# A fused H3 convolution and GLU backward kernel: GLU scratch as contiguous token rows, and the last stage's TensorE work in 128x32 column tiles

## The chip, the cores and the metric

The kernel runs on one core of one Trainium2 chip. The metric is the device time in microseconds (us) of one execution. Three runs of the kernel before took 433.23, 432.94 and 431.38 us; the median is 432.94 us.

## What is computed

The reference is a forward function and its gradient. With 2048 tokens, 512 channels and a GLU width of 1376, the forward function is

```python
xn = layernorm(A_q)
k_shift[s] = sum over t < 4 of k[s - t] * shift_k[:, t]
kv  = k_shift * v
y   = causal_conv(kv, ssm_k) + kv * ssm_D       # by FFT of length 4096
out = A_q + xn * y + ((xn @ w_gate) * (xn @ w_up)) @ w_down
```

The kernel returns `out` and the gradients of the nine inputs for a given `grad_out` (called `go` below): those of q, k, v, the two convolution kernels, `D` and the three GLU weights. Everything is bfloat16, with float32 sums in PSUM.

## The kernel before

The 2048 tokens stand as 16 groups ("rows" r) of 128 partitions. The FFT is written as products with small tables, in three TensorE passes: `a_gen` (weights of 64 rows by 128 columns), `s_B` and `s_Bi` (64x32 and 32x64) and `last_dft` (128x64). Between the passes the data goes through two scratch tensors in device memory, `AX` and `CX`.

The GLU is cut into six steps j of 256 hidden units (one, j = 1, has 96). `mlp_rows` makes, for two token rows at a time, the three products that the gradients need: `h` for `out`, and the gradients of the gate and of the up branch. They lie in SBUF in a ring, 768 values a token (3 parts t of 256), and `dw_gen` makes the weights' gradients of them. The last stage needs the same values with hidden units on partitions, so they are transposed. There are two ways:

- most of them go to the scratch tensor `HD` by `hd_store` (line 440), and come back through DMA transposes issued by `hd_load` (line 616) into two buffers `hdP`, one for each pair of token rows n, in turn. The first four pairs fetch all of `HD`'s columns, the last four leave out one step's.
- step 5 and half of step 4 stay in SBUF and are transposed by TensorE in `turn_gen` (line 602), eight 128x128 blocks for each ScalarE copy back over the ring.

The last stage runs over n = 0..7, each two token rows. `last_dft` (line 693) multiplies what `c_load` (line 646) fetched from `CX` into the one buffer `f["C"]`; its three results go to `c_dkv`, `c_y` and `c_o5`. `c_dsk` (line 738) sums the gradient of the short filter over tokens with eight products of 32 columns. `y_o` (line 759) makes a token row of `out` in 11 products of 128x128 weights with 512 moving columns, and `y_x` (line 777) a row of the gradient of `xn` in 22. VectorE and ScalarE finish the rows, among others in `dk_pair` (the gradient of k).

The order of the work is fixed. Every call of an engine is recorded (class `Eng`, line 143; the recorded function is called in line 173, so the profile gives nearly every instruction this line). `emit` then issues the records in the order that a packed string, `PLAN`, gives, and the same string says which PSUM bank each result gets. Consecutive TensorE calls with the same PSUM bank form one record. All DMAs are issued by SyncE (SP) in one order, so a DMA behind a waiting one waits too. SP's part of the last stage for each n is, in this order: stores of results, `hd_load(n + 2)`, more stores, and the loads of x, k and v and `c_load`, with waits on VectorE, ScalarE and TensorE before many of them.

The DMA transposes of before read rows of 768 values:

```python
HD = dram.tile([R, 640, 768], BF, name="HD")            # line 70
hdP = [place([128, 6, 1152], BF, ...) for i in range(2)] # line 611
ldT(out=hdP[n % 2][:, :, 0:b - a], in_=HP[n, a:b])       # line 618
```

Of the kernel before, what the change touches and what calls it, by code (L numbers as in the profile page):

```python
# [10 lines left out]
BF = mybir.dt.bfloat16  # L11
# [7 lines left out]
D = 512  # L19
F = 1376  # L20
R = 16
NFB = 11
NST = 6
SW = [256, 96, 256, 256, 256, 256]
SF = [0, 1280, 256, 512, 768, 1024]
SB = [0, None, 1, 2, 3, 4]
WO = [12 * sum(SW[:j]) for j in range(NST)]
NCH = 8
KEEP = 8
# [4 lines left out]
KB = 1024  # L34
# [3 lines left out]
def kernel(  # L38
# [24 lines left out]
    nc = tc.nc  # L63
# [3 lines left out]
        return slice(c * 128, (c + 1) * 128)  # L67

    dram = ctx.enter_context(tc.tile_pool(name="dram", bufs=1, space=DRAM))
    HD = dram.tile([R, 640, 768], BF, name="HD")  # L70
    AX = dram.tile([128, 32, 3 * D], BF, name="AX")
    CX = dram.tile([8, 512 * 3 * D + 2048], BF, name="CX")[:, 0:512 * 3 * D]
    KS = dram.tile([128, 12, D], BF, name="KS")
# [66 lines left out]
    def fix(x):  # L140
        return x.at(x.slot.base) if isinstance(x, PV) else x

    class Eng:


        def __init__(self, name, real):
            self.name = name; self.real = real

        def __getattr__(self, meth):
            f = getattr(self.real, meth)  # L150

            def call(*a, **k):
                last = ops[-1] if ops else None
                own = []
                for x in list(a) + list(k.values()):
                    if isinstance(x, PV) and x.slot not in own:
                        own.append(x.slot)
                cols = k["rhs"].shape[-1] if meth == "matmul" and not isinstance(k["rhs"], PV) else 128
                if meth == "matmul":
                    cols = 1  # L160
                    for n in k["rhs"].shape[1:]:
                        cols *= n
                if self.name == "PE" and hold[0]:
                    o = hold[0][0]
                elif (self.name == "PE" and hold[0] is None and last is not None and last.eng == "PE" and last.slots == own
                      and last.cols + cols <= 2200 and last.prio == now[0]):
                    o = last
                else:
                    o = Op(self.name, now[0])
                    ops.append(o)  # L170
                    if self.name == "PE" and hold[0] is not None:
                        hold[0].append(o)
                o.fns.append(lambda: f(*[fix(x) for x in a], **{kk: fix(x) for kk, x in k.items()}))  # L173
                o.uses.append((meth, a, k))
                o.cols += cols
                for s in own:
                    if s not in o.slots:
                        o.slots.append(s)
            return call
# [20 lines left out]
    nc = NC  # L200
# [5 lines left out]
    MM = nc.tensor.matmul  # L206
    ld = nc.sync.dma_start
    st = nc.sync.dma_start
    ldT = nc.sync.dma_start_transpose

    def place(shape, dt, at):
        n = 1
        for s in shape[1:]:
            n *= s
        if dt == BF:
            v = big[0:shape[0], at // 2:at // 2 + n]
        else:
            v = big[0:shape[0], at // 2:at // 2 + 2 * n].bitcast(dt)
        if len(shape) == 3:
            return v.rearrange("p (a b) -> p a b", a=shape[1])  # L220
        if len(shape) == 4:
            return v.rearrange("p (a b c) -> p a b c", a=shape[1], b=shape[2])
        return v
# [23 lines left out]
    ident = rc.tile("ident", [128, 128])  # L247
    W12 = rc.tile("W12", [128, 192])
    W1 = W12[:, 0:128]
    W2 = W12[:, 128:192]  # L250
# [22 lines left out]
    def slot(j, r):  # L273
        return RH + 1536 * ((RO[j] + r) % RING)

    def ring(j, r, n=1):
        if j != 1:
            return place([128, n, 768], BF, slot(j, r)).rearrange("p r (t f) -> p r t f", t=3)
        return place([128, n, 384], BF, slot(1, 0) + 768 * r).rearrange("p r (t f) -> p r t f", t=3)[:, :, :, 32:128]
# [141 lines left out]
        TT(h[:, :, 1:3, :fw], d.to_broadcast((128, 2, 2, fw)), g[:, :, 0:2, :fw], op=ALU.mult)  # L421
        TT(h[:, :, 0, :fw], g[:, :, 0, :fw], g[:, :, 1, :fw], op=ALU.mult)

    HP = HD.rearrange("(n h) p e -> n (h p) e", h=2)

    def hd_at(b, odd):
        return 640 + 128 * b if odd else 128 * ((b + 1) % 4)

    def hd_store(j, r):
        if j == 1:  # L430
            st(HP[r // 2:r // 2 + 2, 512:640].rearrange("n p e -> p n e"), place([128, 2, 768], BF, slot(1, 0) + 768 * r))
        else:
            e, o = hd_at(SB[j], 0), hd_at(SB[j], 1)
            st(HP[r // 2, e:o + 128].rearrange("(h p) e -> p h e", p=128)[:, ::(o - e) // 128, :], ring(j, r, 2).rearrange("p r t f -> p r (t f)"))

    def skb(sk, j, n):
        return sk[:, j, :].unsqueeze(1).to_broadcast((128, n, D))
# [128 lines left out]
    f = {}  # L566
# [26 lines left out]
    def turn_gen():  # L593
        for j, r0 in ((NST - 2, R - KEEP), (NST - 1, 0)):
            blk = [(r, t, b) for r in range(r0, R) for t in range(3) for b in (0, 128)]
            for k in range(0, len(blk), 8):
                pt = bfv(rN(), 8, 128)
                for i, (r, t, b) in enumerate(blk[k:k + 8]):
                    nc.tensor.transpose(pt[:, i, :], ring(j, r)[:, 0, t, b:b + 128], ident[:])
                r, b = blk[k][0], k % 6  # L600
                ACOPY(place([128, 8, 128], BF, slot(j, r) + 256 * b), pt)
                yield
# [5 lines left out]
            for a, b in ((0, 6), (6, 11)):  # L608
                ld(wy[n][:, a:b, :], wy_d[:, i, a:b, :])

    hdP = [place([128, 6, 1152], BF, 109 * KB + 13824 * i) for i in range(2)]

    def hd_span(n):
        return (0, 1152) if 2 * n < R - KEEP else (128, 1024)

    def hd_load(n):
        a, b = hd_span(n)
        ldT(out=hdP[n % 2][:, :, 0:b - a], in_=HP[n, a:b])

    def hd_block(m, t, fb):  # L620
        h = hdP[m // 2 % 2]
        a = hd_span(m // 2)[0]
        if fb == 10:
            return h[:, 3 * (m % 2) + t, 512 - a:640 - a]
        if fb >= 8 or fb >= 6 and m >= R - KEEP:
            return place([128, 6, 128], BF, slot(fb // 2 + 1, m))[:, 2 * t + fb % 2, :]
        c = hd_at(fb // 2, m % 2) - a
        return h[:, 2 * t + fb % 2, c:c + 128]

    def f_alloc():  # L630
        m = Region(RA[0] + 8 * KB, RA[1])
# [62 lines left out]
    def last_dft(n):  # L694
        py = f["py"] = [v3(rF(), 2) for sig in range(3)]
        C = f["C"]
        together()
        for sig in (1, 0, 2):
            for rr in range(2):
                for h in range(2):  # L700
                    MM(py[sig][64 * h:64 * h + 64, rr, :], lhsT=W2, rhs=C[:, 2 * h + rr, sig * D:sig * D + D], start=True, stop=True)
        apart()

    def c_y(n):
# [54 lines left out]
    def y_o(n, rr):  # L759
        m = f["m"][n % 2]  # L760
        end = n == NCH - 1
        for c in (slice(0, 256), slice(256, 512)) if end and rr == 1 else (slice(0, 512),):
            po = rN("y")
            for fb in range(NFB):
                MM(po[:, c], lhsT=hd_block(2 * n + rr, 0, fb), rhs=wy["d"][:, fb, c], start=(fb == 0), stop=(fb == NFB - 1 and not end))
            if end:
                MM(po[:, c], lhsT=ident[:], rhs=m[:, rr, c], start=False, stop=True)
                ACOPY(m[:, rr, c], po[:, c])
            else:
                TT(m[:, rr, c], m[:, rr, c], po[:, c], op=ALU.add)  # L770
        if end:
            st(o0[:, 2 * n + rr, :], m[:, rr, :])
        elif rr == 1:
            st(o0[:, 2 * n:2 * n + 2, :], m[:])

    def y_x(n, rr):
        r = 2 * n + rr
        rs = slice(2 * n, 2 * n + 2)
        px = rN("y")
        for t, w in ((1, "g"), (2, "u")):  # L780
            for fb in range(NFB):
                MM(px, lhsT=hd_block(2 * n + rr, t, fb), rhs=wy[w][:, fb, :], start=(t == 1 and fb == 0), stop=(t == 2 and fb == NFB - 1 and n + 1 < NCH))
        e = t = f["e"][n % 2]; dxn = f["dxn"]
        if n + 1 == NCH:
            MM(px, lhsT=ident[:], rhs=e[:, rr, :], start=False, stop=True)
            nc.scalar.activation(dxn[:, rr, :], px, ACTF.Identity, accum_out=s1[:, r:r + 1])
        else:
            STT(dxn[:, rr, :], e[:, rr, :], 1.0, px, op0=ALU.mult, op1=ALU.add, accum_out=s1[:, r:r + 1])
        STT(e[:, rr, :], dxn[:, rr, :], 1.0, xn[:, r, :], op0=ALU.mult, op1=ALU.mult, accum_out=s2[:, r:r + 1])
        r1 = slice(r, r + 1)  # L790
        TS(c2[:, r1], s2[:, r1], -1.0 / D, None, op0=ALU.mult)
        STT(c1[:, r1], s1[:, r1], -1.0 / D, rstd[:, r1], op0=ALU.mult, op1=ALU.mult)
        STT(dxn[:, rr, :], xn[:, r, :], c2[:, r1], dxn[:, rr, :], op0=ALU.mult, op1=ALU.add)
        nc.scalar.activation(t[:, rr, :], dxn[:, rr, :], ACTF.Identity, bias=c1[:, r1], scale=rstd[:, r1])
        TT(t[:, rr, :], t[:, rr, :], go[:, r, :], op=ALU.add)
        if rr == 1:
            st(o1[:, rs, :], t[:])
# [112 lines left out]
    for n in range(NCH):  # L910
        last = n + 1 == NCH
        t = F0 + n * DF
# [138 lines left out]
```

## Time and profile before

| | |
|---|---|
| median of three runs | 432.94 us |
| span of the profiled execution, first to last instruction | 429.5 us |
| what lies around the span (median less span) | 3.4 us |
| TensorE busy | 419.6 us, 98% |
| VectorE busy | 352.8 us, 82% |
| ScalarE busy | 267.3 us, 62% |
| TensorE instructions | 3174 matmuls and 3174 weight loads |
| mean DMA rate | 290 GB/s |
| DMA packets | 94,878, of which 53,748 under 512 bytes |
| instruction fetch, queue q8 | 25 packets, 0.41 MB |

The profile is of one execution. A "span" is counted from its first instruction, and all times below are on that clock. In a group of the profile, `128*32` before a shape stands for the rows and columns of the weights that the instruction uses, and `128x512` for the partitions and elements that it streams or writes. PEld is the row of weight loads, which run beside the matmuls. SPq is SP's issuing of DMAs: an issue can last long, and nothing behind it is issued meanwhile.

### The profile page before, as it was taken

How to read it: one execution, taken by the hardware profiler on the slowest of the kernel's cores; microseconds unless marked ns; L12 is line 12 of the kernel's file. 1: busy time of each engine (PE TensorE's matmuls, PEld its weight loads, DVE VectorE, ACT ScalarE, POOL GpSimd, SP SyncE). 2: the span in 40 equal slices, each digit the busy share in tenths (PEclk: the TensorE clock that was granted, in tenths of full speed). 3: DMA queues.
4: the chain of work that ended last, by engine and by line, in shares of the span. 5: the costliest groups of instructions: out<-in, count | busy, mean ns of one | idle time of the engine just before them, and what ended most of it. 6: DMA issues, size and time to landing. Idle time of an engine off the chain costs nothing.

```text
span 429.5 us, 8151 instructions
## 1 busy us (share of the span) xinstructions
PE 419.6 (98%) x3174; PEld 204.1 (48%) x3174; DVE 352.8 (82%) x684; ACT 267.3 (62%) x374; POOL 3.5 (1%) x9
## 2 busy tenths in 40 slices
PE   7999999999999999999999999889999999999996
PEld 4665455754454333544444344444444544444443
DVE  6799979998549989899999981044869989999996
ACT  2986879698554998988989963664244340313323
POOL 1000000000000000000000000000000000000000
PEclk9999999999999999999999999999999999999999
DMA  7997787959796979989989989999999999999933
GB/s 249 401 405 240 281 305 264 370 214 381 295 338 200 322 274 306 316 254 338 321 250 315 340 282 254 241 363 336 265 290 267 310 256 317 306 282 301 284 150 124
DMA packets 94878, 124.65 MB, mean 290 GB/s; under 512 B 53748, under 2 KB 63865, under 8 KB 93816
## 3 DMA queue, kind: packets, MB, share of 16 engines
q1 hardware_dynamic: 94840, 124.13, 91.7%
q8 instruction: 25, 0.41, 0.4%
q14 instruction: 13, 0.11, 0.1%
HBM read 57.10 MB, written 54.04 MB: 259 GB/s over the span
## 4 chain that ended last, share of the span: by engine, by line
PE 91%; DMA 6%; DVE 1%; SPq 1%; issue 1%; ACT 0%; ACTq 0%
PE PP L173 91%; DMA big<-CX 4%; DMA big<-in_goT_dram 1%; DVE big L173 1%; SPq L173 1%; ACT big L173 0%; ACTq L173 0%
## 5 line engine op out<-in xcount | busy, mean ns | idle before, releaser
L173 PE MATMUL PP<-big 128*128 128x512 bf16 (+9 forms) x3174 | 419.6, 347 | 5.8 <-issue 1.8
L173 PEld LDWEIGHTS <-big 128*128 128x128 bf16 (+5 forms) x3174 | 204.1, 98 | 221.0 <-issue 65.2
L173 DVE TENSOR_TENSOR big<-big 128x1024 bf16<-128x1024 bf16 (+4 forms) x465 | 269.3, 629 | 46.0 <-ACT big L173 42.6
L173 ACT CAST big<-PP 128x512 bf16<-128x512 f32 (+2 forms) x314 | 225.2, 780 | 90.0 <-PE PP L173 74.8
L173 ACT ACTIVATE big<-big 128x512 bf16<-128x512 f32 (+3 forms) x30 | 19.1, 645 | 40.8 <-DVE big L173 40.8
L173 DVE CAST big<-PP 128x512 bf16<-128x512 f32 (+1 forms) x37 | 32.3, 873 | 11.9 <-PE PP L173 10.0
L173 ACT COPY big<-PP 128x1024 bf16<-128x1024 bf16 x25 | 24.9, 1019 | 21.5 <-PE PP L173 21.5
L173 DVE SCALAR_TENSOR_TENSOR big<-big 128x1 f32<-128x1 f32 (+2 forms) x52 | 25.5, 498 | 0.6 <-ACT big L173 0.2
L173 DVE BATCH_NORM_STATS2 big<-big 128x6 f32<-128x512 bf16 x16 | 10.8, 679 | 2.7 <-DMA big<-in_x_dram 2.6
L173 DVE TENSOR_TENSOR big<-big,PP 128x512 bf16<-128x512 bf16 x14 | 9.5, 682 | 4.1 <-PE PP L173 4.0
L173 DVE SCALAR_TENSOR_TENSOR big<-big,PP 128x512 f32<-128x512 bf16 x14 | 9.5, 682 | 3.3 <-PE PP L173 3.3
L173 DVE TENSOR_SCALAR big<-big 128x1 f32<-128x1 f32 (+1 forms) x28 | 7.0, 259 | 0.2
L173 POOL MEMSET big<- 128x1536 bf16 (+2 forms) x3 | 2.8, 950 | 256.0 <-PE PP L173 252.7
L173 ACT ACTIVATE big<-PP 128x512 f32<-128x512 f32 x2 | 1.2, 598 | 5.5 <-PE PP L173 5.5
L173 DVE RECIPROCAL big<-big 128x2 f32<-128x2 f32 (+1 forms) x9 | 1.4, 155 | 3.7 <-ACT big L173 3.7
L173 DVE BATCH_NORM_AGGREGATE big<-big 128x2 f32<-128x6 f32 x16 | 2.8, 177 | 0.2
L173 ACT ACT_TABLE_LOAD x1 | 1.3, 1283 | 0.7 <-PEq L1039 0.7
L173 DVE DVE_READ_ACCUMULATOR big<-big 128x1 f32 x16 | 1.3, 81 | 0.0
L173 DVE DVE_READ_ACCUMULATOR big<-big,PP 128x1 f32 x14 | 1.1, 81 | 0.0
L173 DVE MEMSET big<- 128x1 f32 (+1 forms) x2 | 0.2, 112 | 0.8 <-PEq L1039 0.8
L173 DVE COPY big<-PP 128x1024 bf16<-128x1024 bf16 x1 | 0.7, 685 | 0.0
L173 ACT ACTIVATION_READ_ACCUMULATOR big<-PP 128x1 f32 x2 | 0.4, 194 | 0.0
(6 smaller groups left out, 0.9 us busy)
## 6 DMA issues: line engine op xcount, KB each, us to landing
HD<-big SPq DMA_DIRECT2D x32, 384.0 KB, 8.2
AX<-big SPq DMA_DIRECT2D x16, 768.0 KB, 5.1
big<-AX SPq DMA_DIRECT2D x16, 768.0 KB, 7.4
CX<-big SPq DMA_DIRECT2D x32, 384.0 KB, 4.5
out_dram<-big SPq DMA_DIRECT2D x44, 256.0 KB, 3.1
big<-CX SPq DMA_DIRECT2D x7, 1536.0 KB, 8.7
big<-in_v_dram SPq DMA_DIRECT2D x16, 256.0 KB, 6.2
big<-in_w_dram SPq DMA_DIRECT2D x4, 768.0 KB, 6.5
```

Of the source, the lines that this page charges most:

```text
L173: o.fns.append(lambda: f(*[fix(x) for x in a], **{kk: fix(x) for kk, x in k.items()}))
```

## The change

There are two edits.

The first is the layout of `HD`. It becomes 16 x 128 rows of 27 x 128 values, one row for each token, 6912 bytes long: three parts of 256 for step 0, three of 128 for step 1, and so on, in columns `HC`. `hd_store` writes pieces of 1536 bytes into these rows (step 1: pieces of 768 bytes, from a store of four token rows, where before it wrote pieces of 1536 bytes). `hd_load` transposes 256 token rows by 27 blocks of 128 columns (21 in the last four pairs) where it transposed 1152 rows by 6 blocks (896 by 6). Both make the same number of 256-byte row pieces: 1152 x 6 = 256 x 27 = 6912, and 896 x 6 = 256 x 21 = 5376. `hd_block` reads the blocks from their new places.

The second is a keyword `part=4` that the recorder understands. It cuts a TensorE call into four, each with 32 columns of the weights and 32 output partitions, with the same moving operand. It is given to all products of `y_o` and `y_x` and to the transposes of step 5 but for the first eight. `last_dft`, with 64 columns, is written as two calls of 32 columns in place of one. `c_dsk` has 32 columns already. The order of the records and `PLAN` stay.

```diff
-    HD = dram.tile([R, 640, 768], BF, name="HD")
+    HD = dram.tile([R, 128, 27 * 128], BF, name="HD")
...
+        @staticmethod
+        def parts(a, k, n):
+            if n == 1:
+                return [(a, k)]
+            w = 128 // n
+            cs = [slice(w * i, w * i + w) for i in range(n)]
+            if "lhsT" in k:
+                h = k["lhsT"].shape[1] // n
+                return [((a[0][w * i:w * i + h],) + a[1:], {**k, "lhsT": k["lhsT"][:, h * i:h * i + h]}) for i in range(n)]
+            return [((a[0][c], a[1][:, c]) + a[2:], k) for c in cs]
...
-                o.fns.append(lambda: f(*[fix(x) for x in a], **{kk: fix(x) for kk, x in k.items()}))
-                o.uses.append((meth, a, k))
+                for aa, kw in Eng.parts(a, k, part):
+                    o.fns.append(lambda aa=aa, kw=kw: f(*[fix(x) for x in aa], **{kk: fix(x) for kk, x in kw.items()}))
+                    o.uses.append((meth, aa, kw))
...
+    HC = {0: 0, 1: 768, 2: 1152, 3: 1920, 4: 2688}
 
     def hd_store(j, r):
         if j == 1:
-            st(HP[r // 2:r // 2 + 2, 512:640].rearrange("n p e -> p n e"), place([128, 2, 768], BF, slot(1, 0) + 768 * r))
+            st(HD[r:r + 4, :, 768:1152].rearrange("r p e -> p r e"), place([128, 4, 384], BF, slot(1, 0) + 768 * r))
         else:
-            e, o = hd_at(SB[j], 0), hd_at(SB[j], 1)
-            st(HP[r // 2, e:o + 128].rearrange("(h p) e -> p h e", p=128)[:, ::(o - e) // 128, :], ring(j, r, 2).rearrange("p r t f -> p r (t f)"))
+            st(HD[r:r + 2, :, HC[j]:HC[j] + 768].rearrange("r p e -> p r e"), ring(j, r, 2).rearrange("p r t f -> p r (t f)"))
...
-                    nc.tensor.transpose(pt[:, i, :], ring(j, r)[:, 0, t, b:b + 128], ident[:])
+                    nc.tensor.transpose(pt[:, i, :], ring(j, r)[:, 0, t, b:b + 128], ident[:], part=4 if j == NST - 1 and k else 1)
...
-    hdP = [place([128, 6, 1152], BF, 109 * KB + 13824 * i) for i in range(2)]
+    hdP = [place([128, 27, 256], BF, 109 * KB + 13824 * i) for i in range(2)]
 
     def hd_load(n):
-        a, b = hd_span(n)
-        ldT(out=hdP[n % 2][:, :, 0:b - a], in_=HP[n, a:b])
+        b = 27 if 2 * n < R - KEEP else 21
+        ldT(out=hdP[n % 2][:, 0:b, :], in_=HD[2 * n:2 * n + 2].rearrange("r p e -> (r p) e")[:, 0:128 * b])
...
-                    MM(py[sig][64 * h:64 * h + 64, rr, :], lhsT=W2, rhs=C[:, 2 * h + rr, sig * D:sig * D + D], start=True, stop=True)
+                    for q in range(2):
+                        o = 64 * h + 32 * q
+                        MM(py[sig][o:o + 32, rr, :], lhsT=W2[:, 32 * q:32 * q + 32], rhs=C[:, 2 * h + rr, sig * D:sig * D + D], start=True, stop=True)
...
     # y_o and y_x: every MM gets part=4
```

In the built program TensorE has 5166 matmuls and as many weight loads, 1992 more of each than before. The order of all other engines' instructions is the same; SP's DMAs differ only in the shapes named above.

More of the change, by code (lines that the diff above doesn't have):

```diff
@@ L153, in call @@
                 last = ops[-1] if ops else None
+                part = k.pop("part", 1)
                 own = []
@@ L422, in mlp_rows @@
         TT(h[:, :, 0, :fw], g[:, :, 0, :fw], g[:, :, 1, :fw], op=ALU.mult)
-    HP = HD.rearrange("(n h) p e -> n (h p) e", h=2)
-    def hd_at(b, odd):
-        return 640 + 128 * b if odd else 128 * ((b + 1) % 4)
+    HC = {0: 0, 1: 768, 2: 1152, 3: 1920, 4: 2688}
     def hd_store(j, r):
         if j == 1:
-            st(HP[r // 2:r // 2 + 2, 512:640].rearrange("n p e -> p n e"), place([128, 2, 768], BF, slot(1, 0) + 768 * r))
+            st(HD[r:r + 4, :, 768:1152].rearrange("r p e -> p r e"), place([128, 4, 384], BF, slot(1, 0) + 768 * r))
         else:
-            e, o = hd_at(SB[j], 0), hd_at(SB[j], 1)
-            st(HP[r // 2, e:o + 128].rearrange("(h p) e -> p h e", p=128)[:, ::(o - e) // 128, :], ring(j, r, 2).rearrange("p r t f -> p r (t f)"))
+            st(HD[r:r + 2, :, HC[j]:HC[j] + 768].rearrange("r p e -> p r e"), ring(j, r, 2).rearrange("p r t f -> p r (t f)"))
     def skb(sk, j, n):
@@ L609, in wy_load @@
                 ld(wy[n][:, a:b, :], wy_d[:, i, a:b, :])
-    hdP = [place([128, 6, 1152], BF, 109 * KB + 13824 * i) for i in range(2)]
-    def hd_span(n):
-        return (0, 1152) if 2 * n < R - KEEP else (128, 1024)
+    hdP = [place([128, 27, 256], BF, 109 * KB + 13824 * i) for i in range(2)]
     def hd_load(n):
-        a, b = hd_span(n)
-        ldT(out=hdP[n % 2][:, :, 0:b - a], in_=HP[n, a:b])
+        b = 27 if 2 * n < R - KEEP else 21
+        ldT(out=hdP[n % 2][:, 0:b, :], in_=HD[2 * n:2 * n + 2].rearrange("r p e -> (r p) e")[:, 0:128 * b])
     def hd_block(m, t, fb):
+        c = slice(128 * (m % 2), 128 * (m % 2) + 128)
         h = hdP[m // 2 % 2]
-        a = hd_span(m // 2)[0]
         if fb == 10:
-            return h[:, 3 * (m % 2) + t, 512 - a:640 - a]
+            return h[:, 6 + t, c]
         if fb >= 8 or fb >= 6 and m >= R - KEEP:
             return place([128, 6, 128], BF, slot(fb // 2 + 1, m))[:, 2 * t + fb % 2, :]
-        c = hd_at(fb // 2, m % 2) - a
-        return h[:, 2 * t + fb % 2, c:c + 128]
+        j = 0 if fb < 2 else fb // 2 + 1
+        return h[:, HC[j] // 128 + 2 * t + fb % 2, c]
     def f_alloc():
@@ L764, in y_o @@
             for fb in range(NFB):
-                MM(po[:, c], lhsT=hd_block(2 * n + rr, 0, fb), rhs=wy["d"][:, fb, c], start=(fb == 0), stop=(fb == NFB - 1 and not end))
+                MM(po[:, c], lhsT=hd_block(2 * n + rr, 0, fb), rhs=wy["d"][:, fb, c], start=(fb == 0), stop=(fb == NFB - 1 and not end), part=4)
             if end:
-                MM(po[:, c], lhsT=ident[:], rhs=m[:, rr, c], start=False, stop=True)
+                MM(po[:, c], lhsT=ident[:], rhs=m[:, rr, c], start=False, stop=True, part=4)
                 ACOPY(m[:, rr, c], po[:, c])
@@ L781, in y_x @@
             for fb in range(NFB):
-                MM(px, lhsT=hd_block(2 * n + rr, t, fb), rhs=wy[w][:, fb, :], start=(t == 1 and fb == 0), stop=(t == 2 and fb == NFB - 1 and n + 1 < NCH))
+                MM(px, lhsT=hd_block(2 * n + rr, t, fb), rhs=wy[w][:, fb, :], start=(t == 1 and fb == 0), stop=(t == 2 and fb == NFB - 1 and n + 1 < NCH), part=4)
         e = t = f["e"][n % 2]; dxn = f["dxn"]
         if n + 1 == NCH:
-            MM(px, lhsT=ident[:], rhs=e[:, rr, :], start=False, stop=True)
+            MM(px, lhsT=ident[:], rhs=e[:, rr, :], start=False, stop=True, part=4)
             nc.scalar.activation(dxn[:, rr, :], px, ACTF.Identity, accum_out=s1[:, r:r + 1])
```

## The prediction

> **What bounds the kernel now.** I read first the page's chain of work that ended last:
>
> ```profile
> PE 91%; DMA 6%; DVE 1%; SPq 1%; issue 1%; ACT 0%; ACTq 0%
> ```
>
> TensorE (PE) sets the time, and DMA in a few places. The same chain in order of time shows which; its columns are start, length and what:
>
> ```profile
> 127.58 148.87 PE PP L173 x1408
> 276.45 1.77 issue
> 278.22 1.50 PE PP L173 x12
> 279.72 0.02 issue
> 279.74 10.12 DMA big<-CX
> 289.86 0.04 issue
> 289.90 102.24 PE PP L173 x595
> 392.14 9.06 DMA big<-CX
> ```
>
> PE streams without a pause from 12 to 276 us. Then three `last_dft` wait for `c_load`. In the trace's records the starts of the matmuls around them lie 2.15, 1.59 and 0.77 us apart where an ordinary entry takes 0.31: 1.84 us lost at 276.4, 1.28 at 288.6, 0.46 at 400.8. Elsewhere products of 512 columns start 216 ns apart, 128 columns 56 ns, 256 columns 109 ns: nothing but streaming. Then the timeline of weight loads around one `c_dsk` and `last_dft`:
>
> ```profile
> 301.81 0.12 PEld L173 LDWEIGHTS <-big 128*32 128x32 bf16 x8 [0.42 <-issue]
> 302.36 1.00 PEld L173 LDWEIGHTS <-big 128*64 128x64 bf16 x12 [0.42 <-issue]
> ```
>
> The loads stop 0.42 us wherever the tile shape changes. By the records, the start of the first matmul after a change lies 309 to 312 ns behind the last one before it, not 216: a change costs 94 ns. Last, busy time by stretches (start, length, then PE, PEld, DVE, ACT, POOL):
>
> ```profile
> 345.00:366.00 21.00, 21.00 (x109) 9.24 (x108) 20.32 (x44) 4.47 (x5) 0.00 (x0) 1.00 1.12 281
> 366.00:385.00 19.00, 19.00 (x100) 8.28 (x98) 18.43 (x39) 5.17 (x6) 0.00 (x0) 1.00 1.07 305
> 402.00:420.00 18.00, 18.00 (x94) 7.95 (x90) 17.89 (x38) 5.45 (x8) 0.00 (x0) 1.00 0.64 185
> ```
>
> The reader is to see three full resources: PE 100%, VectorE (DVE) 97 to 99%, DMA above one. A gain on PE alone does not go through whole.
>
> **Edit 2, the tiles: mode changes.** From `last_dft(0)` at 278.2 us to the end, PE changes shape 26 times. With the edit the weights are 128x32 from `last_dft(1)` on; what stays is into and out of `last_dft(0)` and into `last_dft(1)`. So 23 changes go: 23 x 94 ns = **-2.17 us** on PE.
>
> **Edit 2: the streaming.** Each 512-column product becomes four matmuls and four loads. If the four stream side by side, a round costs 216 ns as now. The rows near to it: in the `c_dsk` bursts (128x32, four tiles) the four start 3 to 4 ns apart and the next round follows 226 ns after the first; 64x32 bursts show 226 too, and the 128x64 bursts, which have six rounds, 240 for the first and 216 for every later one. So the excess belongs to a burst's first round, and one long burst pays it once. A 32-column load takes 94 ns, a 128-column one 98 (groups by shape). I take 0. The ends: below 0, no gain (one 512-column stream cannot be shorter than the 215 ns that every shape shows); above, 10 ns for each of some 580 rounds, +5.8 us.
>
> **Edit 2: the feed.** PE's instructions from `last_dft(1)` on become about 5,500 (690 rounds of 8) in about 132 us of streaming: 24 ns each, 27 in the 512-column parts, 7 in the transposes. The densest stretches of the trace hold 163 PE instructions in 5 us (31 ns) and 282 in 10 us (35 ns), without a pause, so PE's sequencer is shown to be that fast and no limit is seen. I take 0, because no gap between PE's instructions anywhere is put down to it. Upper end: with 35 ns an instruction every round costs 280, +60 us.
>
> A rule of the Trainium skill speaks against this edit: TensorEngine Tiling (Array Packing), Instruction Overhead, gives each matmul some 60 cycles on trn2. At the 2.4 GHz of the skill's TensorE: Matmul & The Clock Gate, four are 100 ns, under 216 for 512 columns but over 56 for a transpose: by it the 88 split transposes would add 88 x 44 ns = 3.9 us. The bursts here, with starts 3 ns apart, show no such cost for tiles side by side.
>
> **Edit 2: instruction fetch.** The page's q8 moved 0.41 MB in 25 packets of 16 KB for PE's 6,348 loads and matmuls. 3,984 more are 16 more packets, all in the last stage, one in each 7 us instead of one in 20. Each keeps one DMA engine about 0.95 us (median of the 25), and a `c_load` or a transpose ends with its slowest engine. I take +0.3 us; the ends are 0 and, if a whole packet falls on the path in each of the three tight periods below, +3.
>
> **What comes back.** The loop after 345 us: the end of `y_x(n, 1)` releases a DMA transpose; SP is held by it; then come four to seven issues of about 0.5 us; then `c_load`; then `last_dft`:
>
> ```profile
> 379.31 10.60 SPq L173 DMA_TRANSPOSE big<-HD  x1
> 389.96 2.09 SPq L173 DMA_DIRECT2D out_dram<-big  x4
> 392.14 0.62 SPq L173 DMA_DIRECT2D big<-CX  x1
> ```
>
> By the packets, the `c_load` data are in 0.3 and 0.2 us ahead of `last_dft(5)` and `(6)`, and `(7)` already waits. So a change of shape removed between a transpose's release and that `last_dft` is not gained. Before 379.3, 15 changes (1.41 us) are gone; `last_dft(7)` comes 1.41 us earlier, not 1.69. Behind it two changes count until the last `y_x` (1.60) and two more until PE's end (1.79). DVE's last chain starts at 420.39 when ScalarE hands it that `y_x`, ends at 426.3, and is 0.45 us behind PE's own: it moves by 1.60. DVE has the idle time for that: its pauses of 1.80 (345.2) to 0.18 us (420.4) are waits for PE. **Sum on the path -1.60**, so +0.57 comes back.
>
> **Edit 1, the layout.** The transposes make the same 256-byte packets, 49,152 in all, and 16 engines took 70 us for them, 22.9 ns a packet on average. A transpose holds SP 7.7 to 11.0 us (mean 9.6), whether it has 6,912 pieces or 5,376: what else is in the queues decides. Where it is on the path: the first one (263.5 to 274.3) stands ahead of the last quarter of `c_load(0)`, which ends the 1.84 us pause; then those before `c_load(5)` to `(7)`. I take **0**, nearest to the row that counts equal packets. Lower end: all hold SP 7.7 us; the 1.84 us pause goes, and some 0.3 at `last_dft(7)`: -2.1. Upper: all hold 11.0: +1.4 at 276 and about 1.2 at three later `last_dft`: +5.
>
> The stores keep pieces of 1536 bytes at 65 ns; step 1's become 1,024 more packets (36 ns for 768 bytes): under 0.5 us of 16 engines. PE's unbroken stream up to 276 us hides it; without this cover it costs those 0.5 us.
>
> A rule for this edit is in the Trainium skill, DMA: Bandwidth & Descriptors, Latency and other measured facts: 261 GB/s for a DMA transpose with a non-contiguous middle dimension, 350 to 400 when contiguous. The second transpose's packets ran from 298.74 to 305.90 us, 1.77 MB, 247 GB/s. At 350 it would take 5.1 us in place of 7.2, and the sum would be -3.4 us in place of -1.3. No run here shows what counts as contiguous.
>
> **Sum.** -2.17 + 0.57 + 0.30 + 0 = **-1.3 us**: span 428.2. The span of 429.5 lies 3.4 us under the median of the runs shown, 432.94; the same 3.4 on top gives **431.6 us**.
>
> **Rivals.**
> - Faster transposes: with 2 us less on SP each, the 276 us pause goes too: -1.3 - 2.1 = -3.4, 429.5. For it: PE, DVE and SP all wait for this first chain. Against: equal packets.
> - Slower than before: the feed. PE's sequencer needs 24 to 27 ns an instruction; it decides from there. At 30 ns, 580 rounds lose 24 ns, 88 transposes 184, 24 rounds of 256 columns 131: 13.9 + 16.2 + 3.1 = +33 us, 464. For it: 27 ns sustained is nowhere in the trace. Against: no pause at 31.
> - Slower DMA: transposes at 11 us or fetch packets on the tight `c_load` path: -1.6 + 5 = +3.4, 436.
> - The change does not do what it says: changes of shape still cost (the four tiles drain between rounds of different PSUM banks), or what PE gains DVE and DMA take: 0, 433.
>
> **How the numbers follow.** Chances: the forecast 0.42 (430.3 to 432.6), faster transposes 0.26, feed 0.12, slower DMA 0.13, nothing 0.07. The likeliest gives 431.6. The range 428.6 to 437 leaves out the feed and a little at both ends. Changes within 0.5% (2.2 us, 430.8 to 435.1) are about what a measurement of this kernel cannot tell from no change. Faster: 0.26 x 0.9 + 0.42 x 0.25 = 0.34. Slower: 0.12 + 0.13 x 0.8 = 0.22. Same: 0.44.
>
> **What would show it.** Right: in the timeline of weight loads one unbroken row of 128x32 behind `last_dft(1)`, rounds 216 ns apart, a q8 of 41 packets, 0.66 MB, DVE still above 97% behind 345 us, waits for `CX` at 276, 288 and 400 us of nearly the same lengths. Wrong: gaps on PE without a releaser (feed), rounds of 226 ns, SP's hold for a transpose moved by over 1 us, or longer waits for `CX` at `last_dft(5)` to `(7)`.

## The result, and the profile after

The changed kernel takes **438.5 us** (median of 16 executions, 432.4 to 444.9); the kernel before, beside it on the same chips, 432.4 (16 executions, 429.0 to 437.8). The ratio is **1.010** (95%: 1.007 to 1.0125): slower by 1%. The median lies above the forecast range of 428.6 to 437; the ratio alone would put the kernel at its upper end, 432.4 x 1.010 = 436.7. Executions over 1.5% above a kernel's fastest are left out of the ratio, six of the 16 here, the profiled one among them; so it is smaller than that of the medians. The profiled execution took 439.9 us, with a span of 438.1 against 429.5: the two spans differ by 8.6 us where the medians differ by 6.1. (Time less span is 1.8 us here; the 3.4 us of the table of before set a median beside the span of one execution.)

First the page: the chain of work by engine, the granted clock, and two rows of the queues.

```profile
PEclk9999999999999999999999999999996999999999
...
q8 instruction: 40, 0.66, 0.6%
q14 instruction: 13, 0.11, 0.1%
...
PE 69%; DMA 16%; DVE 9%; issue 2%; ACT 1%; SPq 1%; ACTq 0%; DVEq 0%
```

DMA rose from 6% of the chain to 16% and DVE from 1% to 9%, PE fell from 91% to 69%. The clock has a dent in one slice. The instruction queue moved the 0.66 MB that were forecast.

At `last_dft(1)` the two programs are still nearly level: PE gets to it at 290.54 us, before at 289.90. So some 8 of the 8.6 us arise behind that. The waits of PE from 275 us on (total, times, longest), before:

```profile
PE PP L173 <- issue: 1.8, 1, 1.8
PE PP L173 <- DMA big<-CX: 1.6, 2, 1.2
```

and after:

```profile
PE PP L186 <- DMA big<-CX: 4.5, 3, 2.2
PE PP L186 <- DMA big<-HD: 4.2, 2, 3.2
PE PP L186 <- issue: 1.2, 3, 0.7
```

Before, PE never waited for `HD`, the transposed GLU values that `y_o` and `y_x` multiply; now it does for 4.2 us. The waits for `CX` rose from 1.6 to 4.5 us, and together with the pauses that are put down to "issue" from 3.4 to 5.7. The chain in order of time, from 300 to 340 us:

```profile
299.82 7.93 PE PP L186 x153
307.75 0.36 issue
308.10 5.60 PE PP L186 x140
313.70 15.88 DMA big<-HD
329.58 0.04 issue
329.62 10.48 PE PP L186 x134
```

One DMA transpose, released by PE at 313.70, landed 15.88 us later. PE had other work until 326.2 and stood still for the last 3.4 us. The transposes as a group show it too (ns: shortest, median, longest hold of SP), before:

```profile
L173 SPq DMA_TRANSPOSE big<-HD x8: 7733/9730/11045, 263.5 to 394.6; - x8
...
DMA to landing us min/median/max: 2.5/8.5/13.2
```

and after:

```profile
L186 SPq DMA_TRANSPOSE big<-HD x8: 8338/10590/12402, 264.5 to 403.0; - x8
...
DMA to landing us min/median/max: 2.6/8.7/15.9
```

The landing row counts the stores to `HD` too; the longest, 13.2 us before and 15.9 after, is a transpose. The timeline of weight loads around that wait (start, length, count, and the pause before):

```profile
308.10 18.10 PEld L186 LDWEIGHTS <-big 128*32 128x32 bf16 x447 [0.53 <-issue]
329.62 0.14 PEld L186 LDWEIGHTS <-big 128*32 128x32 bf16 x8 [3.42 <-DMA big<-HD]
330.02 0.16 PEld L186 LDWEIGHTS <-big 128*32 128x32 bf16 x4 [0.26 <-issue]
330.45 0.16 PEld L186 LDWEIGHTS <-big 128*32 128x32 bf16 x4 [0.26 <-issue]
```

Two things are to be seen. The row of 447 loads has no pause at a change of shape any more: that part of the edit works. And behind the wait the groups of four come 0.43 us apart, not 0.216. The stretches (start and end, length, PE, PEld, DVE, ACT, POOL, clock, DMA share, GB/s) say why:

```profile
326.00:329.50 3.50, 0.38 (x27) 0.20 (x15) 3.36 (x8) 2.62 (x3) 0.00 (x0) 0.84 1.15 349
329.60:335.10 5.50, 5.48 (x52) 2.10 (x56) 2.75 (x5) 0.00 (x0) 0.00 (x0) 0.50 0.93 272
335.20:340.00 4.80, 4.80 (x96) 2.31 (x92) 2.83 (x4) 2.64 (x3) 0.00 (x0) 1.00 1.31 143
```

After 3.46 us without a matmul (from the last start to the next) the granted clock is 0.50 for 5.5 us: 13 rounds take 399 to 427 ns instead of 216, 2.7 us lost. A pause of 2.5 us that ended at 393.5 had no such effect. The Trainium skill warns of this (TensorE: Matmul & The Clock Gate, HAM oscillation): no idle gaps of TensorE over some 3.4 us; the 3.46 here fits. But shorter pauses were followed by it too: near the start of three kernels below, pauses of 2.30 us (`last_dft` alone), 2.56 (full shapes, plain load) and 2.79 (128x32 tiles, plain load) had 3.4 us at a clock of 0.50 at or just behind their end.

Behind 290 us: HD +4.2, clock +2.7, the waits for `CX` there +2.1 (2.5 against 0.4), changes of shape -2.2: +6.8 of the 8.0 us. The rest has no row of its own. The clock's part belongs to this execution: the tiles alone, below, show the waits for `HD` and `CX` with a clock of 1.00 through the whole last stage.

**Why the transposes are late.** The packets of DMA between 313 and 330 us, in 40 slices of 0.425 us:

```profile
GB/s 361 183 99 434 0 181 347 376 463 463 376 318 463 282 235 89 261 289 290 292 313 75 3 10 156 290 302 219 8 164 290 290 290 290 417 371 414 376 313 116
...
q8 instruction: 3, 0.05, 1.2%
q14 instruction: 1, 0.01, 0.1%
```

A transpose runs at 290 GB/s. Within this one the rate falls twice to almost nothing: from 321.9, behind a q8 packet that starts at 321.59, and at 324.9, behind the q14 packet of 324.33. The transpose before it, in stretches of 0.5 us, has a q8 packet that starts at 305.44 and takes 1.17 us:

```profile
305.00:305.50 0.50, 0.50 (x16) 0.24 (x12) 0.50 (x3) 0.30 (x1) 0.00 (x0) 1.00 1.41 319
305.50:306.00 0.50, 0.50 (x16) 0.28 (x12) 0.50 (x2) 0.00 (x0) 0.00 (x0) 1.00 3.98 219
306.00:306.50 0.50, 0.50 (x16) 0.23 (x12) 0.50 (x2) 0.00 (x0) 0.00 (x0) 1.00 0.18 5
306.50:307.00 0.50, 0.50 (x19) 0.23 (x12) 0.50 (x3) 0.00 (x0) 0.00 (x0) 1.00 0.07 7
307.00:307.50 0.50, 0.50 (x20) 0.28 (x13) 0.50 (x2) 0.00 (x0) 0.00 (x0) 1.00 0.32 65
307.50:308.00 0.50, 0.24 (x13) 0.07 (x5) 0.50 (x2) 0.00 (x0) 0.00 (x0) 1.00 1.28 292
```

All 16 engines together move 5 to 7 GB/s for a microsecond: one 16 KB packet, which occupies one engine, stops the transpose on all of them. By the packets that are missing against 290 GB/s such a halt costs 1.3 to 1.5 us, behind a q14 packet of 8 KB (0.31 us) 0.7 to 0.9. In the trace of before it is the same where it happens, here behind the q8 packet of 352.69:

```profile
353.00:353.50 0.50, 0.50 (x4) 0.24 (x3) 0.47 (x1) 0.00 (x0) 0.00 (x0) 1.00 4.54 105
353.50:354.00 0.50, 0.50 (x4) 0.20 (x2) 0.50 (x3) 0.00 (x0) 0.00 (x0) 1.00 0.04 4
354.00:354.50 0.50, 0.50 (x4) 0.24 (x3) 0.50 (x2) 0.00 (x0) 0.00 (x0) 1.00 0.08 9
```

Before, two q8 packets fall inside or at the start of the eight transposes and a third at the very end of one; after the change it is seven, and four more in the last 0.1 us of one. The eight transposes, each from its first packet to its last, take 68.2 us in sum, before 60.7. Five more halts of 1.3 to 1.5 us are 6.5 to 7.5 us, nearly all of it. Ahead of a halt and behind it the transposes run at 290 GB/s in both traces, so four times as many weight loads beside them do not slow them by themselves.

### The profile page after: what moved, and what is told of

Same layout as the page of the kernel before. It is cut to its first block, busy times and chain, and to the rows that moved or that the text cites. A ratio compares the mean times of both kernels' runs of the same rounds, so it can differ in the third digit from the quotient of the medians.

```text
span 438.1 us, 12092 instructions
## 1 busy us (share of the span) xinstructions
PE 416.3 (95%) x5123; PEld 213.2 (49%) x5166; DVE 353.3 (81%) x684; ACT 267.7 (61%) x374; POOL 3.5 (1%) x9
## 4 chain that ended last, share of the span: by engine, by line
PE 69%; DMA 16%; DVE 9%; issue 2%; ACT 1%; SPq 1%; ACTq 0%; DVEq 0%
PE PP L186 69%; DVE big L186 9%; DMA big<-CX 7%; DMA big<-HD 4%; DMA big<-AX 2%; ACT big L186 1%; DMA big<-in_goT_dram 1%; SPq L186 1%; DMA CX<-big 1%; DMA AX<-big 1%; ACTq L186 0%; DVEq L186 0%
## 5 line engine op out<-in xcount | busy, mean ns | idle before, releaser
L186 PE MATMUL PP<-big 128*32 128x512 bf16 (+9 forms) x5123 | 416.3, 351 | 17.7 <-DMA big<-CX 4.5
L186 PEld LDWEIGHTS <-big 128*32 128x32 bf16 (+4 forms) x5166 | 213.2, 98 | 220.5 <-issue 59.2
```

Source lines behind the costliest of these rows:

```text
L186: o.fns.append(lambda aa=aa, kw=kw: f(*[fix(x) for x in aa], **{kk: fix(x) for kk, x in kw.items()}))
```

## The experiments

The theory taken from these rows is **fetch**: 15 more instruction packets, which put seven inside the transposes where there were two, make the transposes late. Its rivals are **the tile shape** (PE itself is slower in 128x32, or the denser weight loads get in the way) and **the layout** (rows of 6912 bytes transpose worse).

The kernels, with before's median beside each and the ratio (95%):

| kernel | us | before | ratio | q8 packets | transposes, ns a packet |
|---|---|---|---|---|---|
| tiles alone | 437.9 | 432.1 | 1.012 (1.008 to 1.016) | 40 | 26.0 |
| layout alone | 432.5 | 432.1 | 1.000 (0.998 to 1.003) | 25 | 22.7 |
| tiles of 64 columns | 434.7 | 432.1 | 1.005 (1.002 to 1.008) | 30 | 24.4 |
| full shapes, plain load | 430.1 | 432.3 | 0.9955 (0.992 to 0.999) | 25 | none |
| 128x32 tiles, plain load | 427.6 | 432.3 | 0.990 (0.9865 to 0.993) | 40 | none |
| memsets on GpSimd | 440.1 | 432.3 | 1.017 (1.0135 to 1.021) | 25 | 22.4 |
| `last_dft` alone in 128x32 | 433.0 | 432.3 | 1.003 (1.000 to 1.006) | 25 | 24.5 |
| split moving operand | 438.0 | 431.7 | 1.014 (1.009 to 1.018) | 37 | 25.7 |
| split, plain load | 431.9 | 431.7 | 1.0006 (0.999 to 1.003) | 37 | none |

Before itself has 25 and 22.9, after 40 and 25.9.

**Tiles alone** has the diff's `Eng.parts`, `part=4` and the new `last_dft`, with before's `HD`, `hd_store`, `hdP` and `hd_load`. **Layout alone** is the reverse:

```diff
-    HD = dram.tile([R, 640, 768], BF, name="HD")
+    HD = dram.tile([R, 128, 27 * 128], BF, name="HD")
```

with the `hd_store`, `hdP` and `hd_load` that go with it.

> The 128x32 tiles alone, on the old HD layout. Theory L (the layout is what costs: in the changed kernel the transposes' packets took 26 ns where they took 22.9, and TensorE waits for HD and CX): this kernel keeps what the tiles give, 23 changes of shape, and is faster than before by 1 to 2 us, about 431. Theory F (the extra instruction fetch, 40 packets of 16 KB in place of 25, is what holds the transposes and c_load up): this kernel is slower than before by 3 to 5 us, with transposes as slow as in the changed kernel, 26 ns a packet.

> The 6912-byte rows alone, all TensorE work as before. Theory L: slower than before by 4 to 6 us, the transposes at about 26 ns a packet and SP held some 0.7 us longer by each. Theory F: the same as before within 1 us, transposes at 22 to 23 ns a packet, q8 with 25 packets.

The loss is whole in the tiles alone. Their profiled execution was the fastest of its six, and yet it has seven q8 packets inside the transposes (67.8 us for the eight in sum) and shows the same halt, behind a q8 packet at 301.95 us (stretches as above):

```profile
302.00:302.50 0.50, 0.50 (x16) 0.28 (x12) 0.50 (x2) 0.00 (x0) 0.00 (x0) 1.00 4.27 222
302.50:303.00 0.50, 0.50 (x16) 0.25 (x12) 0.50 (x2) 0.00 (x0) 0.00 (x0) 1.00 0.32 2
303.00:303.50 0.50, 0.50 (x16) 0.21 (x8) 0.50 (x3) 0.00 (x0) 0.00 (x0) 1.00 0.08 9
```

and PE's waits in the last stage are for the same two:

```profile
PE PP L186 <- DMA big<-CX: 2.4, 2, 2.1
PE PP L186 <- DMA big<-HD: 1.7, 2, 0.9
```

The layout alone is 1.000, and its transposes stay near before's in their hold of SP (median 10.2 us against 9.7, the longest 11.0 in both):

```profile
L173 SPq DMA_TRANSPOSE big<-HD x8: 8301/10199/10976, 263.8 to 396.0; - x8
```

The layout theory falls.

**Tiles of 64 columns** cuts into two instead of four, so that fewer instructions are added; `last_dft` stays as before:

```diff
-... part=4)
+... part=2)
```

> A half dose: the old layout, the last stage's products and the transposes of step 5 cut in two tiles of 128x64, last_dft in 128x64 as before, c_dsk in 128x32. About 620 more matmuls and loads, so some 5 more fetch packets instead of 15; of 23 changes of shape about 8 go (0.8 us). Theory L: 0.5 to 1 us faster than before. Theory F: a third of what the 128x32 tiles cost, so 0 to 1 us slower than before and between before and e1.

Five more packets cost 2.3 us (ratio 1.005), more than the 0 to 1 expected, against 15 more that cost 5.1 (1.012). The loss grows with the count of instructions, but a rival that charges every small tile would say the same.

**Plain loads** take the transpose away: `HD` is fetched by an ordinary DMA of the same bytes (one row of 6912 bytes per partition and token), on the new layout, once with full shapes and once with all the tiles. The values so loaded are not transposed, so `y_o` and `y_x` compute another product, in the same time on PE.

```diff
-        ldT(out=hdP[n % 2][:, 0:b, :], in_=HD[2 * n:2 * n + 2].rearrange("r p e -> (r p) e")[:, 0:128 * b])
+        ld(hdP[n % 2][:, 0:b, :].rearrange("p b q -> p (b q)").rearrange("p (r e) -> p r e", r=2), HD[2 * n:2 * n + 2].rearrange("r p e -> p r e")[:, :, 0:128 * b])
```

> HD is fetched by plain loads of the same bytes, without the transpose, so the last stage multiplies untransposed blocks; all TensorE products in 128x128, 128x64 and 128x32 as before. It is the partner of the next kernel. Theory F (a fetch packet halts a whole DMA transpose, on all 16 engines, for over 1 us) and theory P (the tiles themselves make TensorE or its feed slower) expect the same here: SP is not held, the waits for CX at 276 and 400 us go, 2 to 3.5 us faster than before, about 429.5.

> The same plain loads in place of the transposes, with the 128x32 tiles. Theory F: without transposes a fetch packet delays only its one engine, so the tiles now gain what they save, 23 changes of shape: 1 to 2 us faster than its partner with plain loads and 128x128 products. Theory P: 4 to 6 us slower than the partner, as the tiles were with transposes.

The tiles, slower by 1.2% with transposes, are **faster** without them: 0.990 against 0.9955, 2.5 us (2.0 either way). The 40 packets of instructions are fetched all the same. The same stretch in the two profiles, full shapes first, then tiles:

```profile
345.00:366.00 21.00, 20.89 (x108) 9.23 (x108) 20.51 (x44) 4.47 (x5) 0.00 (x0) 1.00 0.85 292
```

```profile
345.00:366.00 21.00, 21.00 (x395) 16.99 (x391) 20.54 (x45) 4.56 (x5) 0.00 (x0) 1.00 0.87 293
```

Nearly four times the instructions and nearly twice the busy time of weight loads, and PE and DVE are as full as before. So PE is not slower in the small shape. What the tiles cost exists only together with transposes: (1.012 - 1) - (0.990 - 0.9955), from the unrounded ratios 0.0176 of 432.4 us, is **7.6 us**; the three intervals combine to 2.7 either way. The two kernels with plain loads have the new layout, the tiles alone the old; with the changed kernel against the layout alone it is 1.0098 - 1.0002 + 0.0057, 6.6 us. Either number holds the halts and also that part of the tiles' gain which does not come through while PE waits for DMA.

**Memsets on GpSimd** was to add packets of instructions and nothing on PE:

```diff
+                if i == last_pool:
+                    for _ in range(1200):
+                        real.gpsimd.memset(fill[0:1, :], 0.0)
```

> The kernel before, with 1200 one-element memsets on GpSimd behind its last one, so that GpSimd fetches some 10 more packets of 8 KB (queue q14) during the last stage while TensorE's work and instructions stay as they were. Theory F: the transposes slow down with no tile in the kernel, to 24 to 26 ns a packet, with gaps of about 1 us in them where a q14 packet falls, and the kernel is 1 to 4 us slower than before. Theory P: the same as before within 1 us.

It failed as a test. GpSimd needed so long for the 1200 that it ended last (PE's end was at 424.9 us of a span of 437.6; before, PE's end is at 425.4); the chain says so:

```profile
PE 52%; POOL 28%; issue 14%; DMA 4%; SPq 1%; ACT 1%; POOLq 0%; ACTq 0%
```

It added nine q14 packets, of which one fell inside a transpose, at 268.84, and held it up for some 0.6 us; three more came in the first or last moment of one. (The packet at 320.88, which halts a transpose, has its like in before, at 321.15.) The 7.8 us are GpSimd's own work behind PE's end and say nothing on the theories.

**`last_dft` alone** takes the 64-column shape away at a cost of 96 matmuls, without the other tiles; it is the `for q in range(2)` loop of the diff and nothing else.

> Only last_dft in tiles of 128x32, so that it and c_dsk beside it have one shape: 96 more matmuls and loads, under one fetch packet more, and 6 of 26 changes of shape gone. Both theories: 0 to 0.6 us faster than before, the same within what can be measured. A gain of more would say that the tiles pay where they cost few instructions.

A miss: 1.003, an interval that reaches to no change. The count of q8 packets is still 25, but they come at other times: three of them fall into transposes (308.66, 393.65, 410.25), and the transposes need 24.5 ns a packet. That fits the fetch theory, but it was not expected, and one profile is not a proof.

**Split moving operand** adds nearly as many instructions (1,584 matmuls and as many loads, against 1,992) without 128x32 tiles. Each product of `y_o` and `y_x` keeps its 128x128 weights and is cut along the 512 moving columns into four of 128, each with its own weight load:

```diff
+    def M4(out, lhsT, rhs, start, stop):
+        for o in range(0, rhs.shape[-1], 128):
+            MM(out[:, o:o + 128], lhsT=lhsT, rhs=rhs[:, o:o + 128], start=start and o == 0, stop=stop and o + 128 == rhs.shape[-1])
```

It ran with transposes, and with the plain load.

> No tiles: y_o and y_x keep 128x128 weights, old layout, DMA transposes as before, but each product of 512 moving columns is cut into four of 128 columns, each with its own weight load. 1584 more matmuls and loads, 12 more fetch packets in the last stage. TensorE streams 4 x 56 ns in place of 216, 8 ns more for each of some 520 products: +4.2 us by itself. Theory F: the fetch packets halt the transposes as in the tiled kernels, another 3 to 6 us: 8 to 10 us slower than before, about 441, packets of the transposes at 25 to 27 ns. Theory P (it is the 128x32 shape that costs): +4.2 us alone, about 436.5, packets at 23 ns.

> The same cut with plain loads of HD in place of the transposes (the last stage multiplies untransposed blocks). Both theories: TensorE's 4.2 us on top of the kernel with plain loads and uncut products (430.1), so about 434, and faster than its partner with transposes by 2 us (theory P) or by 5 to 8 us (theory F).

With transposes it is as slow as the tiles, 1.014 (438.0 us, between the 436.5 of theory P and the 441 of theory F, with packets of 25.7 ns as F expects); with plain loads 1.0006. The halts are there (a q14 packet at 319.57, a q8 packet at 321.46):

```profile
319.50:320.00 0.50, 0.50 (x13) 0.50 (x10) 0.29 (x1) 0.00 (x0) 0.00 (x0) 1.00 1.27 293
320.00:320.50 0.50, 0.50 (x13) 0.50 (x10) 0.50 (x2) 0.00 (x0) 0.00 (x0) 1.00 2.13 31
320.50:321.00 0.50, 0.50 (x13) 0.50 (x10) 0.50 (x3) 0.00 (x0) 0.00 (x0) 1.00 0.52 110
321.00:321.50 0.50, 0.50 (x13) 0.50 (x11) 0.50 (x3) 0.00 (x0) 0.00 (x0) 1.00 1.38 320
321.50:322.00 0.50, 0.50 (x13) 0.50 (x11) 0.50 (x2) 0.00 (x0) 0.00 (x0) 1.00 4.31 232
322.00:322.50 0.50, 0.50 (x13) 0.50 (x11) 0.50 (x4) 0.00 (x0) 0.00 (x0) 1.00 0.02 2
322.50:323.00 0.50, 0.50 (x13) 0.50 (x11) 0.50 (x1) 0.00 (x0) 0.00 (x0) 1.00 0.09 9
```

and so are waits that before does not have:

```profile
PE PP L173 <- DMA big<-HD: 3.0, 3, 1.3
PE PP L173 <- DMA big<-CX: 2.3, 2, 1.2
```

No 128x32 tile was added here, so the tile shape is not needed for the loss, and that rival falls. What only the pair with transposes costs is 1.0137 - 1 - (1.0006 - 0.9955) = 0.0086, **3.7 us** (2.5 either way), for 12 more packets. The rounds of four do start 223 to 224 ns apart in place of 216, but of PE's own 4.2 us only 2.2 (1.6 either way) came through with plain loads; why was not followed.

Both versions that beat before leave the transposition out; none that computes the whole did.

## Why the prediction was wrong

**The failed step is "Edit 2: instruction fetch".** It counted rightly (41 packets forecast, 40 measured; one in each 7 us) and priced wrongly: a packet was one engine busy for 0.95 us, and a transpose that ends with its slowest engine, so +0.3 us, at most +3. In fact a packet halts a running transpose on all 16 engines for 1.3 to 1.5 us. With eight transposes of 7 to 10 us in 150 us and a packet every 7 us, seven of the eight are hit. They hold SP longer (median 10.6 us against 9.7), so `c_load` behind them starts later, and their own data come too late for `y_o` and `y_x`. By the pairs with and without transposes it is 7.6 us (4.9 to 10.3) in place of 0.3 for this term and 0.57 for what comes back; the two cannot be told apart there. The row that could have told it stood in the trace of before: a transpose with a packet at 352.69 us took 8.4 us, the one after it, with a packet only at its very end, 6.9. One sign of being wrong that the prediction names came true: PE waits 2.17 us for `CX` at 393.5, where before has no wait.

**The rival "slower DMA"** named slow transposes and the fetch packets, but not that the one causes the other, and priced them on the path of `c_load` alone, at 3.4 us with a chance of 0.13. The wait for `HD` and the drop of the clock were in no case, so the range ended at 437.0.

**Mode changes:** right. The row of weight loads is unbroken, and without transposes the tiles gain 2.5 us (2.0 either way) where -2.17 was worked out.

**Streaming and feed:** right at 0. Rounds of 512 columns are 216 ns apart, of 128 columns 56, of 256 columns 109. In the densest 5 us the trace holds 286 PE instructions, 17.5 ns each; the feed, priced at 464 us, is no limit at this rate. The 60 cycles a matmul of the Trainium skill's TensorEngine Tiling (Array Packing), Instruction Overhead, worth +3.9 us, are not to be seen: a transpose in four tiles takes 56 ns, not 100.

**Layout:** right at 0 (1.0002). The 350 to 400 GB/s that the Trainium skill (DMA: Bandwidth & Descriptors, Latency and other measured facts) gives to contiguous transposes were not met by rows of 6912 bytes: the second transpose of the layout alone moved 249.6 GB/s, before 247. Faster transposes, the rival with 0.26, did not occur.

**What comes back (+0.57):** cannot be told apart from the longer waits; it is inside the 7.6 us.

**What stays open.** Which engine carries a fetch was not followed, nor why a halt outlasts the packet (1.3 to 1.5 against 0.95 us). How the loss divides between `HD`, `CX` and the clock is known for one execution of each kernel only; a division that changes would fit the wider spread (12.5 us, before 8.7), but is not shown. Packets moved away from the transposes, with all the tiles kept, were not tried.

## What to carry to other kernels

Count an edit's instructions as traffic: here 3,984 more were 15 packets of 16 KB, and what matters is what runs when one comes. Where DMA transposes run close to the path, ask how long one stands still for a packet, not how long a packet takes on one engine; a transpose in the trace that holds a packet, beside one that does not, gives the price. A kernel with 2.5 us to gain on TensorE lost 4 because its transposes had no slack left.

## What the runs showed of the hardware

- One instruction packet inside a DMA transpose stops its packets on all 16 engines: 1.3 to 1.5 us for 16 KB, 0.7 to 0.9 for 8 KB. Plain loads of the same bytes showed no such loss: with 40 packets, 427.6 us.
- Four 128x32 tiles side by side cost nothing over one 128x128 in streaming (216 ns a round), and save the 94 ns at each change of shape.
- A matmul of 512 columns cut into four of 128 with a weight load each costs little: 7 to 8 ns a product on PE (223 to 224 in place of 216), and 2.2 us (1.6 either way) over 520 products and 24 of 256 columns cut in two (1,584 more weight loads and as many matmuls).
- TensorE idle for 3.46 us was followed by 5.5 us at a granted clock of 0.50, and idle for 2.30, 2.56 and 2.79 us in three other kernels by 3.4 us; idle for 2.5 us ahead of 393.5 was not. A pause between 2.3 and 2.8 us can go either way.
